# A fold that sums over rows s and 272-s before it folds the second axis, and attention reads placed evenly

## The chip, the cores and the metric

The kernel runs on one core of one Trainium2 chip. The metric is the device time of one execution in microseconds (us). Each execution of a kernel gives one time, and one execution of each kernel has a trace from the hardware profiler. Engines are called by the names of the profile: PE is the tensor engine, PEld its weight load, DVE the vector engine, ACT the scalar engine, POOL GpSimd, SP the sync engine. L441 is line 441 of that kernel's source. The changed kernel has three lines more ahead of the later parts, so L608 of the kernel before is L611 after, and L758 is L761.

## The reference

For each of 8 batches, an attention with 32 state rows per head reads in both directions. Its result (544 rows of 512) goes through a Fourier mix over both axes and a two-layer MLP.

```python
def _attn_ref(x, state):                      # x: 8 x 8 heads x 512 x 64, state: 8 x 8 x 32 x 64
    a = softmax(scale * x @ state.T);   xread = a @ state
    a2 = softmax(scale * state @ x.T);  sread = a2 @ x
    return concatenate([xread, sread], axis=2)          # 544 rows

def _moe_ref(x, w_ch1, w_ch2):                # x: 8 x 544 x 512, heads side by side
    mixed = real(fft(fft(x, axis=1), axis=2))
    u = x + mixed
    un = (u - mean(u)) / sqrt(var(u) + 1e-06)
    return u + maximum(un @ w_ch1, 0) @ w_ch2            # 512 -> 2048 -> 512
```

(Shortened: softmax, transposes and the type casts are written out in the original.)

## The kernel before

The kernel is a software pipeline over batches. While PE runs the MLP of batch b (L727 is the first layer, L791 the second), it also runs, in between, the attention reads of batch b+1, then the Fourier mix of batch b+1, and the scores of batch b+2. A helper places the small steps of these streams evenly in a stretch of each stage:

```python
def weave(*streams):
    for n, (steps, lo, hi) in enumerate(streams):
        for i, s in enumerate(steps):
            if s is not None:
                todo.append((lo + (hi - lo) * (i + 0.5) / len(steps), n, i, s))
    ...                                              # sorted by place, then called
...
streams = [(l2_now + ..., 0, 1)]                     # second layer of batch b - 1 and b
    streams.append((layer1(b), 0.13 if b == 2 else 0.08, 1))
    streams.append((reads_next, 0, 0.3))             # the list `second` below, for batch b + 1
    streams.append((transform(b + 1), 0.5 if b == 1 else 0.47, 0.85))
    ...
```

A list of 8 entries therefore has 8 places between 0 and 0.3 of the stage, also where an entry is None. The reads write a PSUM buffer of which there is one (psX, bufs=1), and DVE empties it:

```python
def xread(c0, rev, name, o, ...):
    p = x2(name)                                     # the one PSUM buffer, "xfp" or "xrp"
    for half in range(2):
        nc.tensor.matmul(p[:, half][:, 0:260], lhsT=ET[:, g, c0:c0 + 128], rhs=rhs, ...)      # L441
    nc.vector.reciprocal(rs[ps], p[ps, :, 256:260])                                           # L449
    nc.vector.tensor_tensor(ov, in0=p[...], in1=rs[...], op=ALU.mult)                         # L450: XF or XR
```

The last read of a batch (xrp, rows 256 on) completes the data. The fold then turns XF and XR into XQ, which PE uses as weights:

```python
def fold_rows(k, eng=nc.vector):
    eng.tensor_add(Sm[:, k], XF[:, k], XR[:, k])                                              # L508
    eng.tensor_add(XE[:, k, 0:256], Sm[:, k, 0:256], Sm[:, k, 512:256:-1])                    # L509
    eng.tensor_copy(XE[:, k, 256:257], Sm[:, k, 256:257])                                     # L510

def fold():
    fold_rows(slice(1, 2) if b < 2 else slice(0, 2))
    t = XQ0 if b == 0 else XW
    nc.vector.tensor_add(t[:, 0], XE[:, :, 0:128], XE[:, :, 256:128:-1])                      # L515
    nc.vector.tensor_sub(t[:, 1], XE[:, :, 0:128], XE[:, :, 256:128:-1])                      # L516
    ...                                                                                       # XN, XQl
    nc.vector.tensor_sub(XO[:, :, 1:256], Sm[:, :, 1:256], Sm[:, :, 511:256:-1])              # L526
    nc.vector.tensor_sub(t[:, 2], XO[:, :, 0:128], XO[:, :, 256:128:-1])                      # L527
    nc.vector.tensor_add(t[:, 3], XO[:, :, 128:0:-1], XO[:, :, 128:256])                      # L528
    if b:
        o = XQ.rearrange("p (g j c) -> p g j c", g=2, j=4)
        nc.vector.tensor_add(o[:, 0], XW[:, :, 0], XW[:, :, 1])                               # L531
        nc.vector.tensor_sub(o[:, 1], XW[:, :, 0], XW[:, :, 1])                               # L532
```

For b > 0 the four folds (j = 0 to 3) write an intermediate XW. The last two instructions add and subtract its two row groups, and each of them writes half of all weights (g = 0 or g = 1, every j). The consumer takes the weights by j, both g for each j:

```python
def over_s(j):
    p = qt("gp")
    tab = TC if j < 2 else TS
    for q in range(2):
        ...
        g = 0 if plus else 1
        steps.append((XN[:, g, :] if kind == 4 else Xg[:, g, j, :], t[:, 0, cols]))
        steps.append((XQl[:, j, :], tab[:, 1, cols]))
        for n, (w, t) in enumerate(steps):
            nc.tensor.matmul(p[:, cols], lhsT=w, rhs=t, ...)                                  # L608
```

So over_s(0), which needs a quarter of XQ, can't start before the very last DVE instruction of the fold (batch 5 in the profile: L532 runs from 181.01 for 0.68 us, and over_s(0) starts at 181.75). The order of a batch's reads is:

```python
second = [read_low,
          sread if b < 2 else lambda: xread(0, False, "xfp", XF[:, 0, 0:512]),
          fold_low,
          (...) if b < 2 else sread_by_head,
          (lambda: (fold_rows(slice(0, 1), nc.gpsimd), fold_low_again())) if b < 2 else None,
          lambda: xread(128, False, "xfp", XF[:, 1, 0:512], apart=(b == 0)),
          None,
          lambda: (xread(256, True, "xrp", XR[:, 1, 1:513]), fold())]
```

For b of 2 and more, read_low and the next read stand in neighbouring places, both use the one PSUM buffer, and two of the 8 places are empty.

The softmax here doesn't subtract the row's maximum and nothing guards it: scores larger than these inputs give would overflow.

## Time and profile before

| | before |
|---|---|
| time, median of 3 (then of 4) executions | 318.98 us (318.51 us), 317.99 to 322.14 |
| span of the profiled execution | 318.0 us |
| PE, DVE, ACT, POOL busy | 93%, 56%, 44%, 31% |
| granted PE clock, mean | 0.994 |
| PE's waits after 60 us on the fold / on the reads' buffer | 6.6 us / 2.8 us |
| first read of batch 2 starts at | 63.45 us |

The first row comes from the timed executions, the next three from the page. The waits come from the list of PE's waits, which gives for each instruction that PE stood in front of, what released it, the total in us, how often, and the longest. The lines themselves stand in the prediction below.

### The profile page before, as it was taken

The numbers are of one execution on the slowest core, as the hardware profiler recorded it, in microseconds if no ns is written. First come the engines' busy times: TensorE is split into PE (matmuls) and PEld (weight loads), VectorE is DVE, ScalarE is ACT, GpSimd is POOL, SyncE is SP. The second block draws the span as 40 slices with busy tenths as digits, with TensorE's granted clock in tenths as the row PEclk, the third lists the DMA queues.
The fourth block names the chain that finished last, engine by engine and source line by source line (L and its number), as shares of the span: only waits on it lengthen the run. The fifth ranks groups of instructions, "written<-read, shape, count | busy, mean of one in ns | idle before, by whom it ended". The sixth has DMA issues, their size and how long they took to land.

```text
span 318.0 us, 6056 instructions
## 1 busy us (share of the span) xinstructions
PE 294.4 (93%) x2326; PEld 167.1 (53%) x2326; DVE 179.5 (56%) x440; ACT 140.1 (44%) x267; POOL 97.6 (31%) x219
## 2 busy tenths in 40 slices
PE   4868989987999999999999899998999899999996
PEld 4756977543544455456644354445544444455443
DVE  6595684857385675782924846673846495100112
ACT  5677755744553445234442355234523433343300
POOL 3888674490145022700406012600340022000000
PEclk9999999999899999999999999999999999999999
DMA  8998999045532955348442594253253014600345
GB/s 159 209 202 157 179 169 191 34 85 135 99 87 63 184 115 128 78 97 149 117 101 83 124 175 84 67 115 86 56 111 67 33 35 99 115 35 33 68 118 145
DMA packets 110906, 34.86 MB, mean 110 GB/s; under 512 B 102062, under 2 KB 106414, under 8 KB 110878
## 3 DMA queue, kind: packets, MB, share of 16 engines
q1 hardware_dynamic: 100158, 28.72, 44.1%
q0 software_dynamic: 4224, 4.19, 8.2%
q10 hardware_dynamic: 6496, 1.57, 2.4%
q8 instruction: 18, 0.29, 0.4%
q14 instruction: 10, 0.08, 0.1%
HBM read 22.41 MB, written 14.02 MB: 115 GB/s over the span
## 4 chain that ended last, share of the span: by engine, by line
PE 66%; DVE 18%; issue 5%; DMA 3%; POOL 3%; SPq 2%; ACT 2%; POOLq 0%; DVEq 0%; ACTq 0%
PE po L791 29%; PE ph L727 26%; DMA xs<-in_x_dram 3%; PE gp L608 3%; DVE XR L450 2%; SPq L129 2%; DVE U L567 2%; DVE st L321 1%; DVE XO L526 1%; DVE XE L509 1%; DVE XQ L532 1%; DVE Sm L508 1%; PE xfp L441 1%; PE po L783 1%; POOL xin L132 1%
## 5 line engine op out<-in xcount | busy, mean ns | idle before, releaser
L791 PE MATMUL po<-w,hT 128*128 128x512 bf16 x496 | 125.1, 380 | 0.0
L729 ACT ACTIVATE hT<-ph 128x512 bf16<-128x512 f32 x112 | 66.8, 597 | 122.7 <-PE ph L727 119.8
L727 PE MATMUL ph<-unT,w 128*128 128x512 bf16 x448 | 115.3, 381 | 0.0
L727 PEld LDWEIGHTS <-w 128*128 128x128 bf16 x576 | 50.9, 98 | 47.9 <-issue 0.6
L791 PEld LDWEIGHTS <-hT 128*128 128x128 bf16 x496 | 47.0, 98 | 46.5 <-issue 0.3
L758 DVE SCALAR_TENSOR_TENSOR ot<-po,rstd,U 128x512 f32<-128x512 f32 (+2 forms) x33 | 24.2, 733 | 48.9 <-PE po L791 46.8
L612 POOL COPY GL<-G 128x128 bf16<-128x128 bf16 x8 | 2.3, 291 | 87.5 <-ACT G L609 87.5
L567 DVE TENSOR_TENSOR U<-yp,XR 128x512 f32<-128x512 f32 x16 | 10.9, 684 | 30.5 <-PE yp L563 30.5
L327 POOL TENSOR_TENSOR rstd<-mv,epst 128x1 f32<-128x1 f32 x34 | 8.2, 242 | 46.5 <-DVE mv L323 46.5
L321 DVE BATCH_NORM_STATS2 st<-U 128x6 f32<-128x512 f32 x32 | 21.9, 683 | 0.1
L328 POOL TENSOR_TENSOR rstd<-rstd,mhalf 128x1 f32<-128x1 f32 x34 | 20.4, 601 | 2.7
L609 ACT CAST G<-gp 128x288 bf16<-128x288 f32 x31 | 14.5, 482 | 15.2 <-PE gp L608 15.1
L132 POOL CAST xin<-xs 128x2048 bf16<-128x2048 f32 (+1 forms) x9 | 14.4, 1604 | 7.8 <-DMA xs<-in_x_dram 7.6
L737 PE MATMUL ph<-unT,w 128*128 128x128 bf16 x256 | 16.1, 219 | 0.5 <-ACT unT L648 0.5
L811 PE MATMUL warm<-ident 128*128 128x128 bf16 x144 | 12.0, 232 | 3.7 <-POOL ident masks.py:199 3.6
L737 PEld LDWEIGHTS <-w 128*128 128x128 bf16 x256 | 15.0, 98 | 0.8 <-issue 0.6
L608 PEld LDWEIGHTS <-XQ 128*128 128x128 bf16 x72 | 6.6, 99 | 13.6 <-DVE XQ L532 9.3
L608 PE MATMUL gp<-TC,XQ 128*128 128x144 bf16 x34 | 5.7, 228 | 7.9 <-DVE XQ L532 6.6
L636 DVE TENSOR_SCALAR ub<-U,mv 128x512 bf16<-128x512 f32 x24 | 12.2, 510 | 0.9
L811 PEld LDWEIGHTS <-ident 128*128 128x128 bf16 x144 | 9.9, 105 | 4.1 <-POOL ident masks.py:199 3.6
L450 DVE TENSOR_TENSOR XR<-xrp,rs 128x512 bf16<-128x512 f32 x16 | 11.1, 695 | 1.0 <-POOL XR L281 0.4
L492 POOL COPY XT<-XR 32x514 bf16<-32x514 bf16 x8 | 4.8, 603 | 22.0 <-DVE XR L450 21.7
(190 smaller groups left out, 378.8 us busy)
## 6 DMA issues: line engine op xcount, KB each, us to landing
xs<-in_x_dram SPq DMA_DIRECT2D x22, 256.0 KB, 4.5
w<-in_moe_w_ch_dram POOLq DMA_DIRECT2D x8, 512.0 KB, 9.8
out_dram<-ot SPq DMA_DIRECT2D x15, 256.0 KB, 3.1
r_dram<-ot SPq DMA_DIRECT2D x14, 256.0 KB
out_dram<-r_dram SPq DMA_DIRECT2D x14, 256.0 KB, 3.5
xs<-in_x_dram SPq DMA_DIRECT2D x8, 192.0 KB, 6.3
xs<-in_x_dram ACTq DMA_DIRECT2D x2, 256.0 KB
l_dram<-ot SPq DMA_DIRECT2D x2, 256.0 KB
```

The lines of the kernel that those rows point to most:

```text
L132: copy(xin_bufs[b % 2][:, lo:hi, 1:513], xs_of[b].rearrange("p (i c) -> p i c", i=4)[:, lo:hi])
L321: nc.vector.bn_stats(st6, u)
L328: nc.gpsimd.tensor_tensor(rstd, rstd, mhalf, op=ALU.pow)
L450: nc.vector.tensor_tensor(ov, in0=p[ps, :, 0:256].rearrange("p g (h d) -> p g h d", d=D), in1=rs[ps].unsqueeze(3).to_broadcast([n, 2, 4, D ...
L567: nc.vector.tensor_add(u.rearrange("p (k r) -> p k r", r=2), p.rearrange("p (r k) -> p k r", r=2)[:, 0:u.shape[1] // 2, :], x.rearrange("p ...
L608: nc.tensor.matmul(p[:, cols], lhsT=w, rhs=t, start=(n == 0), stop=(n == len(steps) - 1))
L727: nc.tensor.matmul(ph[:, o:o + n], lhsT=w1[:, c, f * 128:(f + 1) * 128], rhs=un_of[key][:, c, :], start=(c == 0), stop=(c == DC - 1))
L729: nc.scalar.activation(hT[:, per * i:per * i + per, :].rearrange("p a b -> p (a b)"), ph, AF.Relu, scale=-1.0 if key in flipped else 1.0)
L737: nc.tensor.matmul(ph[:, o:o + 128], lhsT=w1[:, c, f * 128:(f + 1) * 128], rhs=un_of[key][:, c, 128 * r:128 * r + 128], start=(c == 0), st ...
L758: nc.vector.scalar_tensor_tensor(ot[:, cols], in0=po_of[i][:, 0:cols.stop - cols.start], scalar=rstd, in1=u[:, cols], op0=ALU.mult, op1=AL ...
L791: nc.tensor.matmul(po_of[i], lhsT=h_of[key][:, f, i * 128:(i + 1) * 128], rhs=w2[:, f, :], start=(f == 0), stop=(f == FC - 1))
L811: nc.tensor.matmul(t[:, 0:128], lhsT=ident, rhs=ident, start=(i == 0), stop=(i == n - 1))
```

## The change

It has two parts. In the **fold**, the sum and the difference over the rows come first (SS), so that every later fold writes finished weights of one j and over_s(0) can start when j = 0 is written. Batch 0 keeps its arithmetic. In batch 1, POOL no longer does its half of XE. In the **spacing**, batches from 2 on get a list of 7 entries with the reads in places 1, 3, 5 and 7 and one None.

```diff
@@ tiles
-    XW = singles.tile([128, 4, 2, 128], F32, name="XW")
+    SS = singles.tile([128, 2, 514], F32, name="SS")
@@ fold
         def fold():
             fold_rows(slice(1, 2) if b < 2 else slice(0, 2))      # now Sm alone, where b > 0
-            t = XQ0 if b == 0 else XW
-            nc.vector.tensor_add(t[:, 0], XE[:, :, 0:128], XE[:, :, 256:128:-1])
-            nc.vector.tensor_sub(t[:, 1], XE[:, :, 0:128], XE[:, :, 256:128:-1])
             if b == 0:
-                nc.vector.tensor_copy(XN[:, :, 0:1], XE[:, :, 128:129])
+                t, o = Sm, XQ0
+            else:
+                t, o = SS, XQ.rearrange("p (g j c) -> p j g c", g=2, j=4)
+                nc.vector.tensor_add(SS[:, 0], Sm[:, 0], Sm[:, 1])
+                nc.vector.tensor_sub(SS[:, 1], Sm[:, 0], Sm[:, 1])
+                even_rows(SS, slice(0, 2))                         # XE and its copy, from SS
+            nc.vector.tensor_add(o[:, 0], XE[:, :, 0:128], XE[:, :, 256:128:-1])
+            nc.vector.tensor_sub(o[:, 1], XE[:, :, 0:128], XE[:, :, 256:128:-1])
+            nc.vector.tensor_copy(XN[:, :, 0:1], XE[:, :, 128:129])
 ... (cut: TN, the two XN adds that go)
-            nc.vector.tensor_sub(XO[:, :, 1:256], Sm[:, :, 1:256], Sm[:, :, 511:256:-1])
-            nc.vector.tensor_sub(t[:, 2], XO[:, :, 0:128], XO[:, :, 256:128:-1])
-            nc.vector.tensor_add(t[:, 3], XO[:, :, 128:0:-1], XO[:, :, 128:256])
-            if b:
-                o = XQ.rearrange("p (g j c) -> p g j c", g=2, j=4)
-                nc.vector.tensor_add(o[:, 0], XW[:, :, 0], XW[:, :, 1])
-                nc.vector.tensor_sub(o[:, 1], XW[:, :, 0], XW[:, :, 1])
+            nc.vector.tensor_sub(XO[:, :, 1:256], t[:, :, 1:256], t[:, :, 511:256:-1])
+            nc.vector.tensor_sub(o[:, 2], XO[:, :, 0:128], XO[:, :, 256:128:-1])
+            nc.vector.tensor_add(o[:, 3], XO[:, :, 128:0:-1], XO[:, :, 128:256])
@@ spacing, b >= 2 (b < 2 stays as it was)
+            second = [read_low, fold_low, read(0, False, XF[:, 0, 0:512]), sread_by_head,
+                      read(128, False, XF[:, 1, 0:512]), None,
+                      lambda: (read(256, True, XR[:, 1, 1:513])(), fold())]
```

More of the change, by code (lines that the diff above doesn't have):

```diff
@@ L508, in fold_rows, with even_rows @@
             eng.tensor_add(Sm[:, k], XF[:, k], XR[:, k])
-            eng.tensor_add(XE[:, k, 0:256], Sm[:, k, 0:256], Sm[:, k, 512:256:-1])
-            eng.tensor_copy(XE[:, k, 256:257], Sm[:, k, 256:257])
+            if b == 0:
+                even_rows(Sm, k, eng)
+        def even_rows(t, k, eng=nc.vector):
+            eng.tensor_add(XE[:, k, 0:256], t[:, k, 0:256], t[:, k, 512:256:-1])
+            eng.tensor_copy(XE[:, k, 256:257], t[:, k, 256:257])
         def fold():
             fold_rows(slice(1, 2) if b < 2 else slice(0, 2))
-            t = XQ0 if b == 0 else XW
-            nc.vector.tensor_add(t[:, 0], XE[:, :, 0:128], XE[:, :, 256:128:-1])
-            nc.vector.tensor_sub(t[:, 1], XE[:, :, 0:128], XE[:, :, 256:128:-1])
             if b == 0:
-                nc.vector.tensor_copy(XN[:, :, 0:1], XE[:, :, 128:129])
+                t, o = Sm, XQ0
[7 more added lines that the diff above has]
+            nc.vector.tensor_copy(XN[:, :, 0:1], XE[:, :, 128:129])
+            if b == 0:
                 for h, t_ in enumerate((TC, TS)):
@@ L521, in fold @@
                     nc.vector.tensor_scalar(TN[:, c], in0=t_[:, 0, c], scalar1=-1.0, scalar2=None, op0=ALU.mult)
-            else:
-                nc.vector.tensor_add(XN[:, 0, 0:1], XE[:, 0, 128:129], XE[:, 1, 128:129])
-                nc.vector.tensor_sub(XN[:, 1, 0:1], XE[:, 0, 128:129], XE[:, 1, 128:129])
             nc.vector.tensor_copy(XQl[32:64, 2, 0:1], XEl[:, 128:129])
-            nc.vector.tensor_sub(XO[:, :, 1:256], Sm[:, :, 1:256], Sm[:, :, 511:256:-1])
-            nc.vector.tensor_sub(t[:, 2], XO[:, :, 0:128], XO[:, :, 256:128:-1])
-            nc.vector.tensor_add(t[:, 3], XO[:, :, 128:0:-1], XO[:, :, 128:256])
-            if b:
-                o = XQ.rearrange("p (g j c) -> p g j c", g=2, j=4)
-                nc.vector.tensor_add(o[:, 0], XW[:, :, 0], XW[:, :, 1])
-                nc.vector.tensor_sub(o[:, 1], XW[:, :, 0], XW[:, :, 1])
+            nc.vector.tensor_sub(XO[:, :, 1:256], t[:, :, 1:256], t[:, :, 511:256:-1])
+            nc.vector.tensor_sub(o[:, 2], XO[:, :, 0:128], XO[:, :, 256:128:-1])
+            nc.vector.tensor_add(o[:, 3], XO[:, :, 128:0:-1], XO[:, :, 128:256])
         if b < 2:
@@ L545, in attend @@
                 first = [turn_state, lambda: turn_x(0), lambda: turn_x(1)] + first
-        second = [
-            read_low,
-            sread if b < 2 else lambda: xread(0, False, "xfp", XF[:, 0, 0:512]),
-            fold_low,
-            (lambda: xread(0, False, "xfp", XF[:, 0, 0:512], apart=(b == 0))) if b < 2 else sread_by_head,
-            (lambda: (fold_rows(slice(0, 1), nc.gpsimd), fold_low_again())) if b < 2 else None,
-            lambda: xread(128, False, "xfp", XF[:, 1, 0:512], apart=(b == 0)),
-            None,
-            lambda: (xread(256, True, "xrp", XR[:, 1, 1:513]), fold()),
-        ]
+        read = lambda c0, rev, o: lambda: xread(c0, rev, "xrp" if rev else "xfp", o, apart=(b == 0 and not rev))
+        if b < 2:
+            second = [read_low, sread, fold_low, read(0, False, XF[:, 0, 0:512]),
+                      lambda: (fold_rows(slice(0, 1), nc.gpsimd), fold_low_again()),
+                      read(128, False, XF[:, 1, 0:512]), None,
+                      lambda: (read(256, True, XR[:, 1, 1:513])(), fold())]
+        else:
+            second = [read_low, fold_low, read(0, False, XF[:, 0, 0:512]), sread_by_head,
+                      read(128, False, XF[:, 1, 0:512]), None,
+                      lambda: (read(256, True, XR[:, 1, 1:513])(), fold())]
         return first, second
```

## The prediction

> **What bounds the kernel now.** I read the page first, then the list of waits of the tensor engine (PE) after 60 us, then the timeline at the places that list named, and last a table of one-microsecond windows. From the page, the busy times of the engines and the one PE group with much idle time before it:
>
> ```profile
> PE 294.4 (93%) x2326; PEld 167.1 (53%) x2326; DVE 179.5 (56%) x440; ACT 140.1 (44%) x267; POOL 97.6 (31%) x219
> ...
> L608 PEld LDWEIGHTS <-XQ 128*128 128x128 bf16 x72 | 6.6, 99 | 13.6 <-DVE XQ L532 9.3
> ```
>
> PE is busy 93% of the span and no other engine passes 56%: the time is PE's work plus PE's gaps. L608 uses the folded rows XQ as weights, and its weight loads stood idle for 13.6 us, 9.3 us of it for L532, the last DVE instruction of a fold. The waits of PE after 60 us (total, times, longest):
>
> ```profile
> PE gp L608 <- DVE XQ L532: 6.6, 5, 2.2
> PE xfp L441 <- DVE XR L450: 2.8, 5, 1.0
> PE tp L645 <- ACT ub L634: 0.3, 1, 0.3
> ```
>
> There are no others. The new fold aims at the first, the spacing of the reads at the second. The timeline of batch 5 (start, length, engine; in brackets idle time and its releaser), first PE, then DVE:
>
> ```profile
> 174.87 0.38 PE L441 MATMUL xrp<-stb,ET 128*128 128x260 bf16 x2
> ...
> 179.41 1.03 PE L791 MATMUL po<-w,hT 128*128 128x512 bf16 x4
> 181.75 0.24 PE L608 MATMUL gp<-TC,XQ 128*128 128x144 bf16 x1 [1.32 <-DVE XQ L532]
> ```
>
> ```profile
> 176.26 0.70 DVE L508 TENSOR_TENSOR Sm<-XF,XR 128x1028 bf16<-128x1028 bf16 x1
> 176.99 0.69 DVE L509 TENSOR_TENSOR XE<-Sm 128x512 f32<-128x512 bf16 x1
> 177.60 0.16 DVE L510 CAST XE<-Sm 128x2 f32<-128x2 bf16 x1
> 177.80 0.43 DVE L515 TENSOR_TENSOR XW<-XE 128x256 f32<-128x256 f32 x1
> ...
> 180.40 0.69 DVE L531 TENSOR_TENSOR XQ<-XW 128x512 bf16<-128x512 f32 x1
> 181.01 0.68 DVE L532 TENSOR_TENSOR XQ<-XW 128x512 bf16<-128x512 f32 x1
> ```
>
> The last read of the batch (xrp) starts at 174.87, the fold runs from 176.26 to 181.70, and PE gets its first weight only at the fold's end. Four 512-column matmuls issue in 0.863 us (the spacing of the groups in this timeline), so the group of 179.41 was out at 180.27 and PE lost 1.48 us; the 1.32 us shown is less, since the ends of pipelined matmuls overlap. The windows around the longest of these waits, in batch 2 (busy PE, PEld, DVE, ACT, POOL, then granted clock):
>
> ```profile
> 77.00:78.00 1.00, 0.00 (x0) 0.00 (x0) 1.00 (x2) 0.00 (x0) 0.00 (x0) 1.00 0.64 195
> 78.00:79.00 1.00, 0.94 (x16) 0.95 (x17) 0.00 (x0) 0.48 (x2) 0.00 (x0) 0.78 0.84 213
> 79.00:80.00 1.00, 1.00 (x7) 0.44 (x5) 0.00 (x0) 0.88 (x3) 0.00 (x0) 0.50 1.26 282
> ```
>
> After 2.2 us without a matmul the clock is halved until about 82; summed over the windows this lost 1.7 us of PE time.
>
> [...]
>
> **The change part by part.**
>
> *DVE work.* Per fold, gone: two XQ adds of 512 (1.38 us by the group means 692 and 685) and two XN adds (0.31). New: two SS adds of 514 (bf16 in, f32 out[...]) and one XN copy (about 0.16, as L510). That saves 0.14 us; over six or seven folds about 1 us of an engine with slack. The arithmetic is not the gain.
>
> *When the first weight is ready.* Before, every weight is finished in the last two instructions. After, the first (j=0, all that the first L608 step needs of XQ) is written by the sixth instruction. By start-to-start distances in the timeline above: Sm to SS 0.73, SS to SS 0.61 (as 531 to 532), SS to XE 0.73 (dependent), XE to its copy 0.61, copy to fold 0.20, fold 0.43: 3.31 us from Sm's start, against 5.44 (176.26 to 181.70). So 2.13 us earlier. The built program's order agrees: each of the four L608 steps may now carry its own wait on DVE, where before only the first had one. Counted from the start of xrp, the first weight moves from 6.87 us (174.87 to 181.74) to 4.74. The second follows 0.34 later and PE asks for it at once only in batches 2 and 3.
>
> *What the spacing moves on PE.* The order of the built programs shows, between xrp and the first L608, this many 512-column matmuls: batch 2, 20 before and 24 after; batch 3, 28 and 32; batches 5, 6, 7, 24 and 32. At 0.216 us each plus 0.22 for xrp, PE has 5.4 us of work in batch 2 after, and 7.1 us in the others. All exceed 4.74, so all five waits vanish. Lost to them were, reckoned as above, 2.34 + 0.63 + 3 x 1.48 = **7.4 us**. For batches 5 to 7 either part should nearly suffice: 24 matmuls last 5.4 us against 4.74 (fold alone), and 32 last 7.1 us against 6.87 (spacing alone). Only batch 2 needs both.
>
> *Second wait.* The reads share one PSUM buffer, so xfp waits until DVE has emptied xrp. By the timelines PE lost 1.03, 0.93, 0.82, 0.34, 0.34 us (batches 2, 3, 5, 6, 7). One more group of four (0.86 us) now stands between. Left: some 0.2 in batch 2, 0.1 in batch 3. Gain **3.2 us**.
>
> *Clock.* Without the gap in batch 2 the half-clock stretch should go: 1.7 us in the profiled run. The three times differ (317.99, 318.98, 322.14; the profiled execution took 319.81), so I take it that not every timed run has it, and count **0.5 us** against the median.
>
> *Unmoved.* No matmul is added or removed; ACT's and SP's order of instructions is the same but for line numbers. In batch 1 POOL loses two instructions and DVE does a little more; PE hardly waits there (its weight load 0.3 us). Stages without reads, from 262 us on, run at full PE and stay.
>
> Sum: 7.4 + 3.2 + 0.5 = 11.1 us at best. I take back 0.6 us for waits that may appear elsewhere: 318.98 - 10.5 = 308.5 us.
>
> **The rivals.**
>
> *A DMA transpose takes over.* PE needs unT (transposed activations) soon after a stage starts. In batch 6's stage the last of four transposes issues at about 198.2 and takes 2.5 us to land (median), 200.7, and the first matmul with it runs at 201.88: 1.2 us of slack, of which the lost xfp wait eats 0.34. Likewise xT in batch 2: the second transpose should land near 75, and the matmul that needs it moves from 78.57 to about 75.4. Both are near but not over. Were both over by 0.5 us in each batch, some 3 us come back: 311.5.
>
> *DVE becomes the bound at the fold.* Then PE would wait at the second or third L608 step instead. Against it: the third step needs XN and j=2, ready near 5.0 us after Sm, and PE asks for it about 2 us after the first; DVE afterwards stands idle 4.9 us in batch 5 until the next yp. Were I wrong by 1 us per fold, 5 us come back: 313.5, within 2%.
>
> *The spacing blocks DVE.* [...] an output add (L758) between two reads could hold a read. Counting groups, the one in front of xrp still follows xfp at once. I expect nothing from it.
>
> *The clock.* If half-clock stretches come and go with chance, either kernel may have one or two more, 1.7 us each: this widens the range, not the centre.
>
> **Range and chances.** Both mechanisms together give 307.9; no spacing gain and some return gives about 312; all gained and the clock never halved gives 306. Range 306.0 to 312.0. Faster by 2% means below 312.6 of 318.98, so half of the expected 10.5 us may be lost before it fails: 0.91 faster, 0.08 same, 0.01 slower.
>
> **What would show it right or wrong.** PE's waits after 60 us on the fold should fall from 6.6 us to under 0.5, those of xfp from 2.8 to under 0.5; PE's busy time stays within 2 us of 294.4 or falls by the half-clock stretch; DVE's busy time falls about 1 us; SS adds last about 0.69 us; the granted clock near 80 us stays 1.0. It would be wrong if PE's list has a new line of several us (a transpose, XN or the second XQ), or if the waits are gone and the span isn't shorter by their sum.

## More of the kernel before

One more view of the kernel before matters for comparison, the chain of waits: the profile walks back from the last instruction, at each step to what released it, and sums the time by engine (a name with q is that engine's queue, which issues; "issue" is time for which the profile shows no wait).

```profile
PE 66%; DVE 18%; issue 5%; DMA 3%; POOL 3%; SPq 2%; ACT 2%; POOLq 0%; DVEq 0%; ACTq 0%
```

DVE is busy 56% of the time, yet 18% of the path that ends last runs over it. A path moves to DVE where PE waits for it, and it stays there until DVE itself was waiting for something. That is the picture of an engine that isn't full but comes late.

## The result

| | before | after |
|---|---|---|
| executions, median | 4, 318.51 us (317.99 to 322.14) | 4, 309.32 us (308.86 to 311.17) |
| ratio after to before, 95% interval | | 0.970 (0.962 to 0.978) |
| profiled span, mean granted clock | 318.0 us, 0.994 | 307.9 us, 0.988 |
| first read of batch 2 starts at | 63.45 us | 65.78 us |
| from there to the end | 254.55 us | 242.12 us |

A ratio is the mean time of one kernel's fast runs over the mean of the other's in the same rounds, so it is not quite the ratio of the medians. All four executions of the changed kernel are marked as fast (an execution is called slow if it is over 1.5% above the fastest of its kernel), and none of either kernel is left out. The median fell by 9.2 us, where 10.5 had been predicted. All outputs are right.

From the page of the changed kernel come the busy times by engine, the granted clock in 40 slices of 7.7 us (tenths of full speed), and the chain of waits.

```profile
PE 293.7 (95%) x2326; PEld 169.8 (55%) x2326; DVE 179.6 (58%) x433; ACT 139.4 (45%) x267; POOL 96.7 (31%) x217
...
PEclk9989988999999999999999999999999999999999
...
PE 82%; DMA 9%; DVE 3%; POOL 2%; SPq 2%; issue 1%; ACT 0%; ACTq 0%; POOLq 0%; DVEq 0%
```

PE's work is the same as before (294.4 us then), and it fills more of a shorter span. The chain says it most plainly: DVE's part of the path fell from 18% to 3% and PE's rose from 66% to 82%. The clock is at 9 (90% or more) from the eighth slice on. It is below that in slices 3, 6 and 7, that is before 54 us, where there is nothing of this change but batch 1's fold. The kernel before had its only slice below 9 at 79.5 to 87.4 us.

PE's waits after 60 us in the changed kernel are the following and no more:

```profile
PE tp L648 <- ACT ub L637: 0.3, 1, 0.3
PE xfp L441 <- DVE XR L450: 0.2, 1, 0.2
```

The line of L611 (L608 before) on the fold, which had 6.6 us, is gone, and the line on the reads' buffer went from 2.8 to 0.2. The next two views are the timeline of batch 5 in the changed kernel, PE first and then DVE (start, length, engine and so on as in the prediction).

```profile
168.19 0.39 PE L441 MATMUL xrp<-stb,ET 128*128 128x260 bf16 x2
...
174.45 1.03 PE L794 MATMUL po<-w,hT 128*128 128x512 bf16 x4
175.31 0.23 PE L611 MATMUL gp<-TC,XQ 128*128 128x144 bf16 x1
```

```profile
169.58 0.70 DVE L508 TENSOR_TENSOR Sm<-XF,XR 128x1028 bf16<-128x1028 bf16 x1
170.31 0.69 DVE L522 TENSOR_TENSOR SS<-Sm 128x514 f32<-128x514 bf16 x1
170.92 0.69 DVE L523 TENSOR_TENSOR SS<-Sm 128x514 f32<-128x514 bf16 x1
171.64 0.69 DVE L513 TENSOR_TENSOR XE<-SS 128x512 f32<-128x512 f32 x1
172.25 0.16 DVE L514 COPY XE<-SS 128x2 f32<-128x2 f32 x1
172.44 0.43 DVE L525 TENSOR_TENSOR XQ<-XE 128x256 bf16<-128x256 f32 x1
```

The first weight (L525) is finished at 172.87, 4.68 us after the read started. PE asks for it at 175.31, 7.12 us after the read, and no bracket stands behind that line: it didn't wait. The margin is 2.4 us. The windows around the place in batch 2 where the clock had halved (busy PE, PEld, DVE, ACT, POOL, then granted clock, share of the DMA engines, GB/s):

```profile
77.00:78.00 1.00, 1.00 (x19) 0.88 (x18) 0.97 (x4) 0.73 (x3) 0.00 (x0) 1.00 0.63 131
78.00:79.00 1.00, 1.00 (x11) 0.51 (x8) 0.95 (x3) 1.00 (x3) 0.00 (x0) 1.00 0.40 81
79.00:80.00 1.00, 1.00 (x10) 0.55 (x8) 0.00 (x0) 1.00 (x3) 0.00 (x0) 1.00 0.53 155
```

There is neither a gap nor a slow clock. The busy time of PE in longer stretches tells where the gain lies. Stages shift a little between the kernels, so the stretches aren't exactly the same work, but a full stretch has no gap left to win:

| stretch, us | 50 to 86 | 86 to 120 | 120 to 160 | 160 to 194 | 194 to 228 | 228 to 262 | 262 to 300 |
|---|---|---|---|---|---|---|---|
| PE busy before | 32.31 | 32.77 | 40.00 | 32.02 | 32.51 | 32.52 | 38.00 |
| PE busy after | 35.49 | 34.00 | 40.00 | 34.00 | 34.00 | 34.00 | 38.00 |

**Where the time went.** From batch 2's first read to the end the profiled execution became 254.55 - 242.12 = 12.4 us shorter. The parts that the prediction named give 7.4 (waits on the fold) + 3.2 (waits on the reads' buffer, with 0.2 left) + 1.7 (the half clock of batch 2, in full since the profiled run had it) = 12.3 us. The span fell by only 10.1 us, as the first read of batch 2 came 2.3 us later (65.78 against 63.45). Whether the change costs these 2.3 us or chance does, the first comparison can't tell.

### The profile page after: what moved, and what is told of

It reads as the page before. It is cut to its first block, busy times and chain, and to the rows that moved or that the text cites.

```text
span 307.9 us, 6048 instructions
## 1 busy us (share of the span) xinstructions
PE 293.7 (95%) x2326; PEld 169.8 (55%) x2326; DVE 179.6 (58%) x433; ACT 139.4 (45%) x267; POOL 96.7 (31%) x217
## 4 chain that ended last, share of the span: by engine, by line
PE 82%; DMA 9%; DVE 3%; POOL 2%; SPq 2%; issue 1%; ACT 0%; ACTq 0%; POOLq 0%; DVEq 0%
PE po L794 35%; PE ph L730 34%; DMA w<-in_moe_w_ch_dram 5%; DMA xs<-in_x_dram 4%; PE gp L611 3%; PE ph L740 2%; SPq L129 2%; PE po L786 1%; PE xrp L441 1%; PE xfp L441 1%; PE yp L566 1%; PE yp L565 1%; POOL xin L132 1%; PE eTp L428 1%; DVE U L570 1%; PE esp L416 1%
## 5 line engine op out<-in xcount | busy, mean ns | idle before, releaser
L732 ACT ACTIVATE hT<-ph 128x512 bf16<-128x512 f32 x112 | 66.8, 597 | 118.1 <-PE ph L730 116.1
L730 PE MATMUL ph<-unT,w 128*128 128x512 bf16 x448 | 113.8, 379 | 0.0
L730 PEld LDWEIGHTS <-w 128*128 128x128 bf16 x576 | 50.7, 98 | 47.0
L328 POOL TENSOR_TENSOR rstd<-rstd,mhalf 128x1 f32<-128x1 f32 x34 | 21.3, 626 | 2.7
L740 PE MATMUL ph<-unT,w 128*128 128x128 bf16 x256 | 17.5, 229 | 0.5 <-ACT unT L651 0.5
L740 PEld LDWEIGHTS <-w 128*128 128x128 bf16 x256 | 16.4, 104 | 0.9 <-issue 0.6
L132 POOL CAST xin<-xs 128x2048 bf16<-128x2048 f32 (+1 forms) x9 | 14.5, 1613 | 7.3 <-DMA xs<-in_x_dram 7.0
L814 PE MATMUL warm<-ident 128*128 128x128 bf16 x144 | 12.4, 235 | 3.7 <-POOL ident masks.py:199 3.6
L639 DVE TENSOR_SCALAR ub<-U,mv 128x512 bf16<-128x512 f32 x24 | 12.3, 514 | 0.9
L742 ACT ACTIVATE hT<-ph 128x512 bf16<-128x512 f32 x16 | 9.3, 598 | 4.7 <-PE ph L740 4.7
L441 PEld LDWEIGHTS <-ET 128*128 128x128 bf16 x64 | 5.6, 98 | 10.3 <-DVE XF L450 3.6
```

The costliest lines, as they stand in the source:

```text
L132: copy(xin_bufs[b % 2][:, lo:hi, 1:513], xs_of[b].rearrange("p (i c) -> p i c", i=4)[:, lo:hi])
L328: nc.gpsimd.tensor_tensor(rstd, rstd, mhalf, op=ALU.pow)
L639: nc.vector.tensor_scalar(t, in0=ud, scalar1=mv[:, 0:1], scalar2=None, op0=ALU.subtract)
L730: nc.tensor.matmul(ph[:, o:o + n], lhsT=w1[:, c, f * 128:(f + 1) * 128], rhs=un_of[key][:, c, :], start=(c == 0), stop=(c == DC - 1))
L732: nc.scalar.activation(hT[:, per * i:per * i + per, :].rearrange("p a b -> p (a b)"), ph, AF.Relu, scale=-1.0 if key in flipped else 1.0)
L740: nc.tensor.matmul(ph[:, o:o + 128], lhsT=w1[:, c, f * 128:(f + 1) * 128], rhs=un_of[key][:, c, 128 * r:128 * r + 128], start=(c == 0), st ...
```

## The experiments

**Theory.** PE waited because the first weight came from the fold's last instruction, and because too little PE work lay between the last read and over_s(0). There is a slack for each batch, PE's work behind the read minus the time to the first weight, and a wait appears only where the slack is negative. Either part raises the slack; batch 2 alone needs both. The half clock of batch 2 (0.50 from 79 us on) follows from the gap of 2.2 us ahead of it; so far that is one gap in one profile.

**Rivals.** (R1) It is the smaller amount of DVE work that counts, not the order of writing. (R2) The gain is the spacing's alone, and the fold adds nothing to it. (R3) The change makes the start slower and pays 2.3 us of the gain for it. (R4) The half clock comes by chance and not from the gap.

Since a start that moves by some 2 us blurs every timed ratio, I give for each kernel also the *segment*: from the start of batch 2's first read to the end of the span, in the profiled execution. It is read from one profile each. How well it repeats can be told for the changed kernel alone: 242.12, 242.08 and 242.15 us in three profiles on different chips.

### The changed kernel again, on two more chips (controls)

There is no edit.

> The changed kernel once more, as the control of this chip. Theory (waits of PE on the fold and on the shared PSUM buffer were the whole gain): 309.3 us plus or minus 1; PE's waits after 60 us together under 1 us. The profiled run lost 2.3 us before batch 2's first read, against the kernel before (65.78 against 63.45 us). If that is chance of the first loads and of the clock, this profile has another place for that read, between 62 and 66 us; rival: the change itself costs it, then it is within 0.5 us of 65.8 again.

> The changed kernel as the control for the next run; the stretch from batch 2's first read to the end 242.1 us within 0.3, as in its two earlier profiles (242.12 and 242.08).

| | median, us (runs) | before in the same rounds | ratio (95%) | first read of batch 2 | segment |
|---|---|---|---|---|---|
| first result | 309.32 (4) | 318.51 (4) | 0.970 (0.962 to 0.978) | 65.78 | 242.12 |
| second chip | 306.66 (6) | 319.78 (11) | 0.961 (0.957 to 0.965) | 62.12 | 242.08 |
| third chip | 306.19 (6) | 319.53 (11) | 0.957 (0.953 to 0.961) | 62.45 | 242.15 |

On two other chips the change is worth 13.1 and 13.3 us by the medians, not 9.2, and my expectation of 309.3 plus or minus 1 us for the second chip was missed. The segment is the same to 0.1 us, so all of the difference lies ahead of batch 2's first read. There the same kernel starts that read at 62.12, 62.45 or 65.78 us, while the kernel before had 63.45. That speaks against R3: the change isn't bound to a late start. But the lateness of the first result isn't one bad execution either: all four of its executions (308.86 to 311.17 us) are slower than all six on the third chip (304.95 to 306.38), while the kernel before was not slower there (318.51 against 319.53). Why the start was late on that chip is not shown. Over all profiles, of whatever kernel, the read starts between 61.6 and 65.9 us.

What precedes a late start can be read from the list of PE's waits between 20 and 64 us. First the run with the read at 65.78, then the one with the read at 62.12:

```profile
PE xfp L441 <- DVE XF L450: 3.1, 1, 3.1
```

```profile
PE xfp L441 <- DVE XF L450: 0.8, 1, 0.8
```

It is a read of batch 1 that waits for the buffer 3.1 or 0.8 us. DVE can't empty it, as an instruction ahead in its queue (L469) waits for POOL's copy of XT (3.1 us in this run, 1.3 us in the kernel before). The copy in turn stands in POOL's queue behind the cast of x for a later batch (L132), and the list of POOL's waits of the late run shows that cast waiting for its load:

```profile
POOL xin L132 <- DMA xs<-in_x_dram: 3.9, 1, 3.9
```

In the early run of the second chip, the list puts the cast's wait down to PE (2.8 us). So in this late run the start hangs on when a load lands. That it does so in general is not shown: of all eleven profiles the list names the load in front of this cast in three (the kernel before, this one, 6 adds more) and a PE instruction in eight, also in late ones. What is common is the path behind the cast: the copy of XT ends between 37.6 and 41.8 us, and the first read of batch 2 follows 23.2 to 24.8 us later. Why the copy comes later in some profiles stays open.

### The fold alone, and the spacing alone

The fold alone puts the old list back into the changed kernel; the spacing alone puts the new list into the kernel before. I compared the built programs: the fold alone moves DVE's and POOL's order only and leaves PE's as before; the spacing alone moves PE's order only.

```diff
 # fold alone: changed kernel with the old list        # spacing alone: kernel before with the new list
-        if b < 2: second = [...]                       -        second = [ ...8 entries... ]
-        else: second = [ ...7 entries... ]             +        if b < 2: second = [...]
+        second = [ ...8 entries... ]                   +        else: second = [ ...7 entries... ]
```

> New fold, old spacing of the reads (PE's instructions stand as before the change). Theory: the first weight is ready 4.74 us after xrp starts, PE has 4.54 us of work in batch 2, 6.3 in batch 3 and 5.4 in batches 5 to 7, so the waits on the fold fall from 6.6 us to under 0.7, while those on the reads' PSUM buffer stay at 2.8. Some 3 us slower than the changed kernel: 312 us. Rival (the spacing does nearly all of it): 6 us or more slower than the changed kernel.

> Old fold, new spacing (DVE's instructions stand as before the change). Theory: the fold's last weights are ready 6.87 us after xrp starts, PE now has 7.1 us of work there in batches 3, 5, 6, 7 and 5.4 in batch 2, so the waits on the fold fall from 6.6 us to about 1.5, all in batch 2, and those on the PSUM buffer to under 0.4. 1 to 2 us slower than the changed kernel: 310.5 us. Rival (the fold does most of it): the waits on the fold stay above 4 us, 313 us or more.

| | median, us (runs) | ratio to before (95%) | segment | gain in the segment |
|---|---|---|---|---|
| fold alone | 309.86 (5) | 0.969 (0.967 to 0.972) | 245.73 | 8.8 |
| spacing alone | 310.77 (6) | 0.971 (0.968 to 0.974) | 244.37 | 10.2 |
| both, same chip | 306.66 (6) | 0.961 (0.957 to 0.965) | 242.08 | 12.5 |

PE's waits after 60 us of the fold alone, and below those of the spacing alone:

```profile
PE xfp L441 <- DVE XR L450: 2.8, 5, 1.0
PE po L794 <- issue: 0.6, 4, 0.2
PE tp L648 <- ACT ub L637: 0.3, 1, 0.3
```

```profile
PE gp L608 <- DVE XQ L532: 1.7, 1, 1.7
...
PE xfp L441 <- DVE XR L450: 0.2, 1, 0.2
```

The list of the fold alone has no wait on the fold left, and the waits on the reads' buffer stand as before (2.8 us). (In batch 2 PE's first product starts 4.74 us after the read, 74.74 against 70.00, where the 20 matmuls between last 4.54 us by the prediction's reckoning. So some 0.2 us were lost there, too little for the list to show.) The spacing alone has only batch 2's left, 1.7 us long, and next to none on the buffer. R2 falls, and so would its mirror image. The gains 8.8 and 10.2 add up to 19.0 and not to 12.4, as they overlap: in batches 3 and 5 to 7 each part alone removes the wait on the fold, and in both profiles the half clock of batch 2 (1.7 us) is gone. Which part is worth more the timed runs don't tell: their ratios, 0.969 and 0.971, are the same within the intervals. Together they are worth more than either, by 3.7 us over the fold alone (the buffer's waits above all) and by 2.3 us over the spacing alone (1.7 of wait shown, some more lost).

Where the spacing alone has its last wait, DVE's timeline in batch 2 shows something that I had not expected:

```profile
71.53 0.75 DVE L758 SCALAR_TENSOR_TENSOR ot<-po,rstd,U 128x512 f32<-128x512 f32 x1 [0.67 <-PE po L791]
72.20 0.20 DVE L449 RECIPROCAL rs<-xrp 128x8 f32<-128x8 f32 x1
72.43 0.69 DVE L450 TENSOR_TENSOR XR<-xrp,rs 128x512 bf16<-128x512 f32 x1
```

With the new spacing an output add (L758) lands on DVE just in front of the last read's reciprocal. (The order on DVE is not new: in the kernel before, the add stands there too, but it was done at 71.26, and the reciprocal started 0.43 us after the read's matmuls at 71.17.) The reciprocal starts 0.87 us after the read's matmuls (71.33), where in batch 5 of the changed kernel it takes 0.42 (168.19 to 168.61). In the full change the same happens, and the first weight of batch 2 is out 5.13 us after the read there, against 4.68 in batch 5. PE's 24 matmuls last 5.40 us, so nothing is lost, but the margin of batch 2 is 0.3 us and not 0.7.

### The same arithmetic, the first weights written last

This has the new fold with the old list, but writes j = 1 and then j = 0 at the fold's end.

```diff
-            nc.vector.tensor_add(o[:, 0], XE[:, :, 0:128], XE[:, :, 256:128:-1])
-            nc.vector.tensor_sub(o[:, 1], XE[:, :, 0:128], XE[:, :, 256:128:-1])
+            if b == 0:
+                ...                                     # the same two, batch 0 only
 ...
             nc.vector.tensor_add(o[:, 3], XO[:, :, 128:0:-1], XO[:, :, 128:256])
+            if b:
+                nc.vector.tensor_sub(o[:, 1], XE[:, :, 0:128], XE[:, :, 256:128:-1])
+                nc.vector.tensor_add(o[:, 0], XE[:, :, 0:128], XE[:, :, 256:128:-1])
```

> New fold with the same instructions, old spacing, but the two folds of XE that give the first two weights are written last. Theory (what counts is when the first weight is ready): it is ready 5.4 us after Sm starts, as before the change (5.44), so PE's waits on the fold are back at 6 to 7 us and the time is that of the kernel before within 1 us, some 318. Rival (the gain of the fold is its smaller arithmetic): as fast as the new fold with the old spacing, some 312 us.

PE's waits after 60 us:

```profile
PE gp L615 <- DVE XQ L539: 5.9, 5, 2.0
PE xfp L441 <- DVE XR L450: 2.8, 5, 1.0
```

The median is 317.18 us of 6 runs, against 319.78 of before; the ratio 0.994 (0.990 to 0.998). The 2.6 us between the medians are more than the 1 us that I allowed, but in the profile most of such a difference lies ahead of the first read of batch 2 (61.57 us here, 63.45 before). The segment is 253.73 us, 0.8 less than before and 8.0 more than the fold alone, whose instructions it has. The five waits are back at 5.9 us in place of 6.6, which is 0.14 us less each: that is what the smaller arithmetic is worth. The experiment decides against R1. The order of writing is the fold's gain, and it is about ten times the value of the saved work.

### Delaying the first weight by a known amount

If a slack decides, a delay of the first weight must cost nothing until it is used up, and then cost its excess. The changed kernel writes the first SS add 4 or 7 times for batches from 2 on.

```diff
-                nc.vector.tensor_add(SS[:, 0], Sm[:, 0], Sm[:, 1])
+                for _ in range(4 if b > 1 else 1):      # 7 in the other kernel
+                    nc.vector.tensor_add(SS[:, 0], Sm[:, 0], Sm[:, 1])
```

> The changed kernel with the first SS add written four times instead of once in batches 2 to 7: three more DVE instructions of 0.61 us start to start, 1.83 us ahead of the first weight. Theory (PE has 7.1 us of own work between the last read and the first fold product in batches 3, 5, 6, 7 and 5.4 us in batch 2, against a first weight at 4.74 us): the slack is 2.4 us, in batch 2 only 0.7, so PE waits only in batch 2, 1.0 to 1.3 us, and the stretch from batch 2's first read to the end grows from 242.1 us to about 243.3. Rival (the fold is on the path in each batch): six times 1.83 = 11 us longer.

> As delay3, with the SS add written seven times: 3.66 us more. Theory: waits of about 3.0 us in batch 2, 1.3 in batches 3, 5, 6 and 7 and 0.5 in batch 4, lost 8.7 us together, and the gap in batch 2 halves the clock again, 1.7 us: the stretch from batch 2's first read to the end 251 to 253 us. Rival (each batch pays in full): 22 us longer, 264. Rival (slack is larger than reckoned): under 248.

| | median, us (fast runs) | ratio to before (95%) | segment | PE's waits on the fold |
|---|---|---|---|---|
| 3 adds more | 309.96 (3) | 0.970 (0.965 to 0.975) | 244.59 | 1.8, in one batch |
| 6 adds more | 322.56 (4) | 1.011 (1.006 to 1.015) | 257.03 | 12.2, in six batches |

(A fourth run of the first, 315.41 us, was slow and is left out.) PE's waits on the fold after 60 us, with 3 adds more and with 6 more:

```profile
PE gp L612 <- DVE XQ L526: 1.8, 1, 1.8
```

```profile
PE gp L612 <- DVE XQ L526: 12.2, 6, 4.0
```

I had counted 0.61 us for each add, the distance of SS to SS; but adds that write the same region again stand 0.73 apart (four of them last 2.88 us in the trace), about as an add does that reads the output of the one before (0.72, SS to XE in batch 5 above). The kernel with 3 adds more, batch 2:

```profile
71.91 0.39 PE L441 MATMUL xrp<-stb,ET 128*128 128x260 bf16 x2
...
74.47 2.88 DVE L523 TENSOR_TENSOR SS<-Sm 128x514 f32<-128x514 bf16 x4
...
79.28 0.24 PE L612 MATMUL gp<-TC,XQ 128*128 128x144 bf16 x1 [1.81 <-DVE XQ L526]
```

So the delays were 2.19 and 4.38 us. With these, and a first weight at 5.18 us in batch 2 (an estimate from the timelines, 4.74 plus the 0.44 by which the output add holds the read up) and 4.74 in the others, the slack gives:

| | PE's work behind the read | 3 more: first weight, loss | 6 more: first weight, loss |
|---|---|---|---|
| batch 2 | 5.40 | 7.37, **1.97** | 9.56, **4.16** |
| batches 3, 5, 6, 7 | 7.12 | 6.93, 0 | 9.12, **2.00** each |
| batch 4 | 8.02 | 6.93, 0 | 9.12, **1.10** |
| sum | | **1.97** | **13.26** |

The times of the first weight can be read off the timelines too, as PE takes it at once where it waits (0.05 us after L526 ends at 79.23): 7.37 us behind the read with 3 adds more (79.28 - 71.91), and 9.56 us in batch 2 and 9.12 us in each other batch with 6. The shown waits are 1.8 and 12.2 us. A shown wait is some 0.17 us shorter than the time that PE lost, as in the prediction (1.32 shown, 1.48 lost), since the group of four matmuls ahead is shown as 1.03 us long where such groups start 0.86 us apart: 1.8 + 0.17 = 1.97 and 12.2 + 6 x 0.17 = 13.2. Both fit. The segments say the same: 244.59 is 2.5 us over the changed kernel's 242.1 (0.5 more than the wait; I have no reason for that rest), and 257.03 is 14.9 over it, 13.2 of waits and 1.7 of a half clock, which came with the 4.0 us gap. I had expected 251 to 253 us for the second, and missed because of the 0.73. A delay of 2.19 us cost nothing in five of six batches, and twice that cost something in all six. A model in which each batch pays for the delay in full would have asked for some 13 us from the first.

### Does the gap slow the clock?

The kernel before gets 30 small matmuls on data at hand in the gap of batch 2, ahead of over_s(0). They change no result; PE just has work (the 30 last 1.84 us in this kernel's profile).

```diff
+            t = transform(b + 1)
+            if b == 1:
+                t[0] = lambda s=t[0]: (warm(30), s())
-            streams.append((transform(b + 1), 0.5 if b == 1 else 0.47, 0.85))
+            streams.append((t, 0.5 if b == 1 else 0.47, 0.85))
```

> The kernel before with 30 more 128x128 matmuls on the identity (1.7 us of work) in PE's gap of 2.3 us ahead of batch 2's first fold product. Theory (the gap itself halves the clock): the granted clock stays 1.0 there and the stretch from batch 2's first read to the end falls from 254.55 us by 1.7 to about 252.9, though nothing waits less. Rival (the clock falls by chance or by another cause): it falls in this stretch again, 254.5 us or more, and the added matmuls give nothing.

The windows around the filled gap in the profile (columns as above):

```profile
77.00:78.00 1.00, 0.50 (x10) 0.33 (x7) 0.68 (x2) 0.00 (x0) 0.00 (x0) 1.00 0.91 273
78.00:79.00 1.00, 0.95 (x17) 0.76 (x16) 0.00 (x0) 0.81 (x3) 0.00 (x0) 1.00 0.93 212
```

The 30 matmuls fill the gap but for half a microsecond at 77, and the clock stays at 1.00. PE does the first weight's work at the same time as before, so only the clock can gain. The segment is 253.08 us, 1.5 less than before, where 1.7 was expected. The timed ratio is 0.999 (0.995 to 1.002), so it doesn't resolve a gain of that size: a start that varies by more than 2 us hides it. R4 has this against it, and the gaps of the other profiles: a gap of 2.0 us (the first weights written last) was followed by the windows

```profile
76.00:77.00 1.00, 0.95 (x10) 0.96 (x11) 0.00 (x0) 0.32 (x1) 0.00 (x0) 0.58 0.77 205
77.00:78.00 1.00, 1.00 (x12) 0.65 (x10) 0.00 (x0) 0.99 (x3) 0.00 (x0) 0.50 1.24 281
```

and gaps of 2.2 (before) and 4.0 us (6 adds more) by half clock too; gaps of 1.7 (spacing alone) and 1.8 us (3 adds more) were not. That is six profiles in one order, each seen once. But the record holds more, and it does not bear out a limit near 2 us:

- Near 20 us, in the work of batch 0, PE has the same gaps in all ten profiles in which this place wasn't edited: 1.1 to 1.2 us, 0.8 us soon after, and in most a third of 0.6 us. In six of them a half clock sets in behind these gaps, between 20 and 24 us (all three of the changed kernel, the fold alone, the spacing alone, the first weights written last; 0.50 to 0.69 in the lowest window of 2 or 4 us), in four none does: the kernel before (1.00 from 20 to 28 us), before with the filled gap (mean clock 1.000) and both delays, these by their mean clock (0.993 and 0.989), which leaves room for no more stretches than the one of the next point and, with 6 adds more, the one behind the gap of 4.0 us. (The spacing alone has one more stretch, between 8 and 16 us: 0.73 and 0.84 in windows of 4 us.)
- A gap of 3.1 to 4.1 us near 43 us occurs in four profiles (the changed kernel's first, 3 and 6 adds more, and the next experiment) and a half clock goes with it. In the changed kernel, after a gap that ends at 43.25 us, the windows from 44 to 48 us show 0.64 and 0.51; in the next experiment those from 42 to 46 show 0.55 and 0.60. For the two delays (4.1 and 3.3 us) it is put here by the mean clock alone.
- Each stretch at half clock in these profiles costs 1.7 us (in the kernel before 0.22, 0.50, 0.50 and 0.49 us in the windows from 78 to 82 us, so 3.4 us at half rate), which takes 0.005 off the mean granted clock of an execution, and that mean is on record for every timed run. Of the 33 control executions of the kernel before, four have 0.999 or 1.000, so no such stretch at all, with the gap unfilled (these executions have no trace). Of the six with the filled gap, four have 1.000.

So a half clock came with gaps: with the five of 3.1 to 4.1 us between PE's work every time (in two of them by the mean clock alone), and with shorter ones of 0.6 to 2.2 us sometimes. The 3.6 us ahead of PE's very first matmul were not followed by one (1.00 up to 16 us in the kernel before and in the changed one), nor were the other four waits on the fold in the kernel before (0.5 to 1.3 us, 1.00 behind each). As far as these counts go, R4 is wrong in that the gap matters, and right in that chance has a part: the same gaps are followed by it in one execution and not in another. That the gap of batch 2 slowed the clock is well supported and not proved.

### Can the start be made faster by more warm-up?

In the changed kernel's controls the clock is halved around 22 to 25 us. If the gaps there bring that on, more filler ahead of that place keeps the clock up. In the profiles 70 of these matmuls in a row last 4.07 us and the control's 48 last 2.84 us, so 22 more are 1.2 us of work.

```diff
-          ([lambda: warm(44)], 1, 1))
+          ([lambda: warm(66)], 1, 1))
```

> The changed kernel with 66 instead of 44 warming matmuls between batch 0's last read and its first fold product (1.2 us more of work in a PE gap of 1.2 us), to keep the half-clock stretch near 20 us away; from batch 2's first read on PE is already full, so the start is where time is left. If the gap is the cause as it was in batch 2: no half clock between 19 and 26 us and up to 1 us faster than the control. Rival: the gap is too short to matter or the added matmuls hold up PE when DVE is early: same time within 0.5 us, or slower.

The half clock near 22 us is gone in the profile (1.00 from 20 to 25 us, where the control on the same chip has 0.70). But another stands from 42 to 46 us, where the control has none. First this run, then the control, mean clock in the third column from the end:

```profile
38.00:46.00 8.00, 4.28 (x49) 3.82 (x47) 3.19 (x10) 2.92 (x7) 6.28 (x10) 0.79 1.29 159
```

```profile
38.00:46.00 8.00, 6.61 (x109) 6.17 (x107) 5.47 (x14) 4.10 (x10) 6.44 (x12) 1.00 1.50 181
```

Either profile lost 1.7 us to the half clock in all, so nothing was gained there. The kernel is slower than that control: 308.57 us of 6 runs against 306.19 of 6, with a segment of 242.32 us. The first read of batch 2 starts at 64.88 instead of 62.45, and PE's longest wait between 20 and 64 us is

```profile
PE xfp L441 <- DVE XF L450: 3.7, 1, 3.7
```

which is the late start of above (in this profile the list puts the cast's wait of 3.7 us down to PE, not to the load), and the half clock sets in at the end of that gap. So this run doesn't tell what a start without half clock would give. All six executions (306.67 to 309.03 us) are slower than all six of the control (304.95 to 306.38), so something in this program costs time; how the 22 more matmuls do it, I didn't settle. The changed kernel remains the best version.

## Why the prediction was right

The text put 308.5 us; measured were 309.32, and 306.66 and 306.19 on other chips, all in its range. That the first lies so near the forecast is partly luck: from batch 2's first read on the gain was 12.4 us, 1.9 more than the 10.5 forecast, and the start, for which the prediction had no term, took 2.3 back. By its steps:

- **First weight earlier.** Right. It said 4.74 us after the read's start. In batch 5 the write is finished after 4.68, and in the fold alone, where PE waits for it in batch 2, PE takes it after 4.74. The SS adds last 695 and 687 ns, where the text had 0.69 us; the add of the kernel before with the same types (L509, bf16 in and f32 out, 512 elements) lasts 695 ns.
- **The waits on the fold vanish, and most by either part alone.** Right. The waits went from 6.6 us to none; fold alone none; spacing alone only batch 2. "Only batch 2 needs both" was nearly wrong: there the fold alone left some 0.2 us, the spacing alone 1.7. The runs with delays showed that the reckoning of slack is right to about 0.1 us in each batch, with the length of the delay taken from their traces; as forecast it was too short.
- **The waits on the reads' buffer fall to 0.2 and 0.1.** Right: 0.2 is shown, and the spacing alone does it.
- **The clock near 80 us.** Right that it stays at 1.00. The 0.5 us counted against the median was a compromise, and the profiled segment gained the whole 1.7.
- **0.6 us taken back for waits elsewhere.** Not needed: no line of the list after 60 us is new in the first profile (that of the second chip has four stops of up to 0.2 us without a releaser, 0.6 in all), no transpose took over, and XN is in time.
- **DVE's busy time falls by 1 us.** Half right. The rows of the fold's instructions sum to 44.3 us before and 43.3 after, so the saving is there. (By the rows of the kernel before, 1.38 and 0.31 us go, and two adds like L509 and a copy like L510, 1.39 and 0.16 us, come: the 0.14 us per fold of the text.) The engine's busy total is 179.5 and 179.6 all the same, perhaps since it counts overlapping instructions once and other rows moved by some tenths; I did not add this up. The term was sized by rows and looked for in the total, where it doesn't show. Its worth on the path, when the weights come last, is 0.14 us per batch.
- **"I expect nothing" from an output add in DVE's queue ahead of a read.** Off. It holds the last read of batch 2 for 0.4 us. In the full change it costs no time, since it eats a margin of 0.7 us; in the spacing alone it lengthens the wait.
- **The spread of the timed runs put down to the half clock.** This step was wrong, and it is the reason why the first measured gain was 9.2 and not 12.4 us. What varies most is when the first read of batch 2 starts, 61.6 to 65.9 us; in the late profile of the first result it came behind a load of x. The number of half-clock stretches doesn't follow it closely: on the second chip two executions of the kernel before with the same mean clock (0.993 and 0.994) took 318.19 and 320.75 us. The prediction looked at nothing ahead of 60 us and so had no term for this. The sum of the mechanisms was right for the part that the change touches, and where the start was early (second and third chip) the whole gain shows.
- **Two sums.** "Half of the expected 10.5 us may be lost" before a gain of 2% fails: from 308.5 to 312.6 it is 4.1 us, so four tenths. And "all gained and the clock never halved gives 306" comes to 306.7 by the text's own terms (318.98 - 7.4 - 3.2 - 1.7). Neither bore on the outcome.

## What to carry to other kernels

When an engine that isn't full delays the full one, look at which of its instructions writes what the consumer needs first, and reorder so that each write is a finished, separately waited-for piece: here the same arithmetic in another order was worth 8 us of 318 (1.7 of it a half clock that went with the gap), the saved arithmetic 0.8. Reckon a slack for each place (work of the consumer behind the trigger minus time to the first piece), because two remedies for one wait don't add (here 8.8 and 10.2 us alone made 12.5 us together), and the place with the least slack tells whether both are needed (here batch 2, where the fold alone had 4.54 us of PE's work against 4.74 to the first weight, and both parts had 5.40 against 5.13). And compare the segment that the change touches between profiles, not only whole times, when an unrelated start moves by a quarter of the gain.
